# A six-layer cross network in bf16: the first layer as one sequence of twelve half-blocks

## The chip, the cores and the metric

The kernel runs on one core of a Trainium2 chip. The core has a matrix engine (TensorE, PE in the profile, with its weight loads shown as PEld), VectorE (DVE), ScalarE (ACT), GpSimd (POOL) and SyncE (SP), which here only issues DMAs. Engines run on their own instruction streams and wait for one another by semaphores. The metric is the device time of one execution in microseconds (us); lower is better.

## The reference

```python
B, F, D, L = 4096, 26, 16, 6          # Din = F * D = 416
x = x0                                 # (4096, 416) bf16
for l in range(6):
    x = x0 * (x @ ws[l] + bs[l]) + x   # ws (6, 416, 416), bs (6, 416)
return x
```

Each layer is a 4096x416 by 416x416 product, a bias, an elementwise product with the input and a sum.

## The kernel before

The data lie transposed: features on the 128 partitions, batch along the free dimension. The 416 features are three blocks of 128 (`m` as output block, `k` as input block) and a rest of 32. The batch is two parts `s` of 2048 columns, each part four groups of 512 (`g`), and a half `h` of a part is two groups (`gl` = 0, 1). A half-block (s, m, h) is 128 features by 1024 columns; it fills one PSUM tile [128, 2, 512] in fp32. The PSUM pool has four such buffers, which is the whole of PSUM, so a new tile waits until an older one has been read out.

The recurrence is kept as a running sum. In layer 0, `x0*(x0@W + b) + x0 = x0*(x0@W + b + 1)`, so 1 is added to layer 0's bias, `CM` holds the bracket, and `XH` holds `CM * XM0`, the next input. In a later layer the product is evicted into `t`, `CM += t`, and `XH = CM * XM0`. `CR`, `XR` are the same for the 32 rest features. There the four column groups of a part are stacked on the 128 partitions: partitions 32g to 32g+31 hold group g.

TensorE uses three shapes. A full product is 128x128 by 512 columns (layer 0, L240). A column-tiled product loads 32 output columns of the weights; four of them, on different quarters of the array, run side by side (layers 1 to 4, L208, and the rest features' output, `pr`, L220 and L224). A row-tiled product contracts only the 32 rest features; four of them, on partitions 0, 32, 64 and 96 of `XR` or `XRd`, run side by side (L214, and L247 in layer 0). `XRd` is `XR` with its halves of partitions swapped, so that the block m = 1 can use the other two quarters. Each 512 columns of a half-block take three full products (k = 0, 1, 2) and one row product.

Inputs. Eight DMA transposes on SP's queue bring `XM0` (512 columns each, in the order (s, g)). ScalarE's queue issues layer 0's weights, the biases, four pieces `xrig` (the rest columns of s = 0, turned by TensorE in `x0_rem0`), the rest rows of layer 0's weights `WR` (one quarter, copied to the other three by ScalarE twice and GpSimd once, L118 and L120), and `xrem` (the rest columns of s = 1, 2048 rows of 64 bytes, L91), which VectorE turns in `x0_rem1` (L172, L174). A memset of one column of `xrem` (L89), which VectorE does after the copies in `x0_rem0`, sets the moment at which this load is issued, since the DMA overwrites that column.

Order. Within an engine the order comes from the tile framework's scheduler, except where `pin` (keep in program order) fixes it. Layer 0 is `first_layer(s)`, called for s = 0 and s = 1. In each call the three half-blocks of h = 0 get their full products, then one group of eight row products runs (four half-blocks: (0,h=0), (0,h=1), (2,h=0), (1,h=0)), then the products of h = 1, then a group of four row products, so layer 0 has four row groups: eight, four, eight, four. For s = 0 the full products of half 0 are split around the four TensorE transposes of `x0_rem0`. At the end come the 32 products of `pr`. ScalarE evicts every tile (L181 in layer 0, L187 later, L194 and L197 for the rest); VectorE does all sums and products (L183, L188, L189, L198, L201).

Layers 1 to 4 take the tiles (s, m) two by two: 12 column-tiled steps, eight row products (closing one tile and opening the next), 12 steps; after the first pair comes the rest (`rem_pair`). The last layer works with the batch on partitions and writes the output; `xl_rem` copies the rest columns of the running sum, brought by a DMA transpose into `scrR`, for it.

Of the kernel before, what the change touches and what calls it, by code (L numbers as in the profile page):

```python
# [16 lines left out]
def kernel(  # L17
# [7 lines left out]
    nc = tc.nc  # L25
# [62 lines left out]
    def load_xrem1():  # L88
        pin(nc.vector.memset(xrem[:, 0, 0:1], 0.0))  # L89
        with nc.allow_non_contiguous_dma(reason="64B row segments"):  # L90
            pin(nc.scalar.dma_start(xrem[:], x0[SW:2 * SW, NK * P:D].rearrange("(p t) r -> p t r", p=P)))  # L91
# [23 lines left out]
    for g in range(1, NG):  # L115
        dst, src = WR[32 * g:32 * g + 32, 0, :], WR[0:R, 0, :]
        if g < NG - 1:
            nc.scalar.copy(dst, src)  # L118
        else:
            nc.gpsimd.tensor_copy(dst, src)  # L120
# [20 lines left out]
    fill_wd(0, 1)  # L141
    fill_wd(1, L)
# [33 lines left out]
    def ew_main(l, s, m, h, pt, nxt):  # L176
        c0 = col0(s, 2 * h)
        c, x = CM[:, m, c0:c0 + 2 * CW], nxt[s][:, m, 2 * CW * h:2 * CW * h + 2 * CW]
        src, bias = pt[:].rearrange("p a b -> p (a b)"), bM[:, m, l:l + 1]
        if l == 0:  # L180
            nc.scalar.activation(c, src, ACT.Identity, bias=bias, scale=1.0)  # L181
            for a in range(0, 2 * CW, CW):
                pin(nc.vector.tensor_tensor(out=x[:, a:a + CW], in0=c[:, a:a + CW],  # L183
                                            in1=XM0[:, m, c0 + a:c0 + a + CW], op=ALU.mult))
            return
        t = tpool.tile([P, 2 * CW], BF16, name="t")
        nc.scalar.activation(t[:], src, ACT.Identity, bias=bias, scale=1.0)  # L187
        nc.vector.tensor_tensor(out=c, in0=t[:], in1=c, op=ALU.add)  # L188
        nc.vector.tensor_tensor(out=x, in0=c, in1=XM0[:, m, c0:c0 + 2 * CW], op=ALU.mult)  # L189

    def ew_rem(l, s, pr, nxtR):
        cols = slice(CW * s, CW * s + CW)
        if l == 0:
            nc.scalar.activation(CR[:, cols], pr, ACT.Identity, bias=bR[:, 0:1], scale=1.0)  # L194
        else:
            tr = tpool.tile([P, 2 * CW], BF16, name="t")
            nc.scalar.activation(tr[:, 0:CW], pr, ACT.Identity, bias=bR[:, l:l + 1], scale=1.0)  # L197
            nc.vector.tensor_tensor(out=CR[:, cols], in0=tr[:, 0:CW], in1=CR[:, cols], op=ALU.add)  # L198
        for a in range(CW * s, CW * s + CW, CW if l else CW // 2):
            part = slice(a, a + (CW if l else CW // 2))  # L200
            prod = nc.vector.tensor_tensor(out=nxtR[:, part], in0=CR[:, part], in1=XR[0][:, part], op=ALU.mult)  # L201
            if l == 0:
                pin(prod)
# [14 lines left out]
    def mm_rem(l, s, pr, cur, curR):  # L218
        for g in range(NG):
            nc.tensor.matmul(pr[32 * g:32 * g + 32, :], lhsT=WD[:, l, g, :], rhs=curR[:, CW * s:CW * s + CW],  # L220
                             start=True, stop=False, tile_position=(0, 32 * g))
        for k in range(NK):
            for g in range(NG):
                nc.tensor.matmul(pr[32 * g:32 * g + 32, :], lhsT=WM[:, l, k, NK * P:D], rhs=cur[s][:, k, CW * g:CW * g + CW],  # L224
                      start=False, stop=(k == NK - 1), tile_position=(0, 32 * g))
# [8 lines left out]
    def first_layer(s):  # L234
        cur, curR, nxt, nxtR = XM0, XR[0], XH, XR[1]

        def full(pt, m, h, gl, after_row):
            c0 = col0(s, 2 * h + gl)
            for k in range(NK):
                nc.tensor.matmul(pt[:, gl, :], lhsT=WM[:, 0, k, 128 * m:128 * m + 128], rhs=cur[:, k, c0:c0 + CW],  # L240
                                 start=(k == 0 and not after_row), stop=(k == NK - 1 and after_row))

        def row(pt, m, h, opens):
            for gl in range(2):
                rg = 32 * ((2 * h + gl) ^ (2 if m == 1 else 0))
                src = XRd if m == 1 else curR
                nc.tensor.matmul(pt[:, gl, :], lhsT=WR[rg:rg + 32, 0, 128 * m:128 * m + 128],  # L247
                                 rhs=src[rg:rg + 32, CW * s:CW * s + CW],
                                 start=opens, stop=not opens, tile_position=(rg, 0))
# [3 lines left out]

        pa = [ph(m) for m in range(NK)]
        if s == 0:
            for m in range(NK):
                full(pa[m], m, 0, 0, False)
            tp0 = psum.tile([P, CW + 8], BF16, tag="ps", name="tpr")
            x0_rem0(tp0[:])
            for m in range(NK):  # L260
                full(pa[m], m, 0, 1, False)
        else:
            for gl in range(2):
                for m in range(NK):
                    full(pa[m], m, 0, gl, False)
        pb = [ph(0)]
        row(pa[0], 0, 0, False)
        row(pb[0], 0, 1, True)
        row(pa[2], 2, 0, False)
        row(pa[1], 1, 0, False)  # L270
        for m in range(NK):
            ew_main(0, s, m, 0, pa[m], nxt)
        for m in range(NK):
            if m:
                pb.append(ph(m))
            for gl in range(2):
                full(pb[m], m, 1, gl, m == 0)
        row(pb[1], 1, 1, False)
        row(pb[2], 2, 1, False)
        if s == 0:  # L280
            x0_rem1()
            for m in range(NK):
                ew_main(0, s, m, 1, pb[m], nxt)
            return
# [3 lines left out]
        for m in range(2):  # L288
            ew_main(0, s, m, 1, pb[m], nxt)
        ew_rem(0, 0, pr[:, 0, :], nxtR)  # L290
        ew_main(0, s, 2, 1, pb[2], nxt)
        ew_rem(0, 1, pr[:, 1, :], nxtR)
# [3 lines left out]
    for s in range(NS):  # L296
        first_layer(s)
# [10 lines left out]
    def xl_rem(s):  # L308
        tc.keep_in_program_order(
            nc.scalar.copy(XLrows[:, 16 * s:16 * s + 16, NK * P:D].rearrange("p (g i) r -> p i g r", g=NG),  # L310
                           scrR[s][:].rearrange("p i (g r) -> p i g r", g=NG)))
# [159 lines left out]
```

## Time and profile before

| | |
|---|---|
| time, median of 3 runs | 130.42 us (130.15 to 130.46) |
| the profiled execution's own time | 130.23 us |
| its span | 128.1 us |
| TensorE, matmuls | 123.5 us busy (96%), 1708 instructions |
| VectorE | 100.9 us (79%) |
| ScalarE | 86.2 us (67%) |
| GpSimd | 4.8 us (4%) |
| L208, column-tiled products | 65.2 us busy, 1152 instructions |
| L240, full products of layer 0 | 16.3 us busy, 379 ns each |
| L247, row products of layer 0 | 1.4% of the chain that ended last |

The page gives busy time by engine, the span in 40 slices (each digit is tenths of a slice, PEclk the clock granted to TensorE), the DMA queues (q1 is SP's, q10 ScalarE's), the chain of work that ended last, and the costliest groups of instructions. Matmuls overlap one another: a product of 512 columns is shown with 379 ns, but the next begins after a shorter step, so the step between starts is what counts. A timeline line gives start, length of the merged stretch, engine, line, operation, operands and count. "DMA to landing" is counted from the start of the issue.

### The profile page before, as it was taken

To read this page: it belongs to the slowest core of one execution; us is meant where nothing else is said; L and a number is where in the kernel's file an instruction comes from. 1 tells how busy PE (TensorE), PEld (TensorE's weight loads), DVE (VectorE), ACT (ScalarE), POOL (GpSimd) and SP (SyncE) were. 2 spreads that over 40 slices of the span, in tenths; PEclk is the share of its full clock that TensorE was granted. 3 is DMA by queue.
4 is the path that set the end of the run, shared out by engine and by line. 5 is a ranking of instruction groups with operands and counts; after the bars stand their busy time and mean duration, and the time that the engine had idled before them with its cause. 6 is when DMAs were issued, how large, how long until landed. Compare 5 with 4: busy or idle time off the path is not lost.

```text
span 128.1 us, 4002 instructions
## 1 busy us (share of the span) xinstructions
PE 123.5 (96%) x1708; PEld 55.9 (44%) x1710; DVE 100.9 (79%) x195; ACT 86.2 (67%) x98; POOL 4.8 (4%) x18
## 2 busy tenths in 40 slices
PE   7999999999999999999999999999999999999980
PEld 3343343444434444434444434444434445445450
DVE  0123579964979898989898989898989899988991
ACT  0048857878848668848668848668849696569660
POOL 4004001300000000000000000000000000000000
PEclk9999999999999999999999999999999999999999
DMA  3999999999940000000000000000498899976764
GB/s 93 234 234 224 174 238 259 318 332 336 336 144 0 5 0 0 8 0 5 0 5 0 5 0 5 0 0 5 86 125 192 161 135 236 199 231 220 228 194 142
DMA packets 42229, 16.37 MB, mean 128 GB/s; under 512 B 31034, under 2 KB 42212, under 8 KB 42212
## 3 DMA queue, kind: packets, MB, share of 16 engines
q1 hardware_dynamic: 37432, 15.40, 53.3%
q10 hardware_dynamic: 4780, 0.72, 3.6%
q8 instruction: 13, 0.21, 0.7%
q14 instruction: 4, 0.03, 0.1%
HBM read 6.15 MB, written 3.41 MB: 75 GB/s over the span
## 4 chain that ended last, share of the span: by engine, by line
PE 92%; DMA 4%; DVEq 1%; ACT 0%; issue 0%; DVE 0%
PE pt L208 50%; PE ph L240 13%; PE py L365 12%; PE pt L214 5%; PE pr L224 5%; DMA XM<-in_x_dram 4%; PE pr L220 2%; PE py L377 1%; PE ph L247 1%; PE py L380 1%; PE py L359 1%; DVEq L466 1%; PE tpr L163 1%; ACT t L405 0%; PE py L369 0%
## 5 line engine op out<-in xcount | busy, mean ns | idle before, releaser
L208 PE MATMUL pt<-XH,WM 128*32 128x512 bf16 x1152 | 65.2, 379 | 0.0
L187 ACT ACTIVATE t<-pt,bM 128x1024 bf16<-128x1024 f32 x48 | 49.6, 1115 | 19.3 <-PE pt L214 19.3
L208 PEld LDWEIGHTS <-WM 128*32 128x32 bf16 x1152 | 29.7, 97 | 33.8 <-issue 5.1
L188 DVE TENSOR_TENSOR CM<-t,CM 128x1024 bf16<-128x1024 bf16 x48 | 32.9, 686 | 5.1 <-ACT t L187 5.1
L189 DVE TENSOR_TENSOR XH<-CM,XM 128x1024 bf16<-128x1024 bf16 x48 | 33.2, 692 | 3.6
L405 ACT CAST t<-py 128x416 bf16<-128x416 f32 (+1 forms) x22 | 14.3, 649 | 5.1 <-PE py L365 2.0
L365 PE MATMUL py<-WM,XH 128*128 128x416 bf16 x90 | 17.0, 339 | 0.0
L240 PE MATMUL ph<-XM,WM 128*128 128x512 bf16 x70 | 16.3, 379 | 0.2
L181 ACT ACTIVATE CM<-ph,bM 128x1024 bf16<-128x1024 f32 x12 | 12.5, 1113 | 3.5 <-PE ph L247 3.5
L183 DVE TENSOR_TENSOR XH<-CM,XM 128x512 bf16<-128x512 bf16 x24 | 9.1, 438 | 3.6 <-ACT CM L181 3.6
L365 PEld LDWEIGHTS <-XH 128*128 128x128 bf16 x90 | 8.5, 98 | 7.6 <-issue 1.4
L240 PEld LDWEIGHTS <-WM 128*128 128x128 bf16 x72 | 6.8, 97 | 8.6 <-issue 1.1
L407 DVE TENSOR_TENSOR t<-t,XLrows 128x416 bf16<-128x416 bf16 (+1 forms) x20 | 9.3, 467 | 1.1 <-ACT t L405 1.1
L395 DVE TENSOR_TENSOR o<-t,X0rows 128x416 bf16<-128x416 bf16 (+1 forms) x22 | 9.9, 456 | 0.1
L214 PE MATMUL pt<-XR,WR 32*128 32x512 bf16 x96 | 7.3, 379 | 0.0
L224 PE MATMUL pr<-XH,WM 128*32 128x512 bf16 x96 | 6.6, 379 | 0.0
L197 ACT ACTIVATE t<-pr,bR 128x512 bf16<-128x512 f32 x8 | 5.1, 683 | 2.1 <-PE pr L224 2.1
L114 ACT ACT_TABLE_LOAD x1 | 1.3, 1283 | 6.1 <-DMA XM<-in_x_dram 6.1
L201 DVE TENSOR_TENSOR XR<-CR,XR 128x512 bf16<-128x512 bf16 (+1 forms) x12 | 4.4, 379 | 1.1 <-ACT CR L194 0.8
L224 PEld LDWEIGHTS <-WM 128*32 128x32 bf16 x120 | 3.2, 97 | 3.2
L148 PE MATMUL wps<-const-float32-1.0 128*128 128x512 f32 x4 | 3.8, 1094 | 0.8 <-PEq L455 0.8
L157 DVE CAST bM<-pb 128x18 f32<-128x18 bf16 x1 | 0.2, 177 | 4.9 <-PE pb L156 4.9
(52 smaller groups left out, 47.2 us busy)
## 6 DMA issues: line engine op xcount, KB each, us to landing
X0rows<-in_x_dram SPq DMA_DIRECT2D x8, 312.0 KB, 6.7
out_dram<-o SPq DMA_DIRECT2D x9, 208.0 KB, 3.2
WM<-in_ws_dram SPq DMA_DIRECT2D x5, 312.0 KB
out_dram<-o SPq DMA_DIRECT2D x13, 104.0 KB, 1.7
X0rows<-in_x_dram SPq DMA_DIRECT2D x4, 208.0 KB, 6.1
WR<-in_ws_dram SPq DMA_DIRECT2D x4, 130.0 KB, 4.8
WM<-in_ws_dram ACTq DMA_DIRECT2D x1, 312.0 KB
XM<-in_x_dram SPq DMA_TRANSPOSE x8, 5.7
```

Source lines behind the costliest of these rows:

```text
L181: nc.scalar.activation(c, src, ACT.Identity, bias=bias, scale=1.0)
L187: nc.scalar.activation(t[:], src, ACT.Identity, bias=bias, scale=1.0)
L188: nc.vector.tensor_tensor(out=c, in0=t[:], in1=c, op=ALU.add)
L189: nc.vector.tensor_tensor(out=x, in0=c, in1=XM0[:, m, c0:c0 + 2 * CW], op=ALU.mult)
L208: nc.tensor.matmul(pts[g // 2][32 * q:32 * q + 32, g % 2, :], lhsT=WM[:, l, k, 128 * m + 32 * q:128 * m + 32 * q + 32], rhs=cur[s][:, k, C ...
L214: nc.tensor.matmul(pts[g // 2][:, g % 2, :], lhsT=WR[32 * g:32 * g + 32, l, 128 * m:128 * m + 128], rhs=curR[32 * g:32 * g + 32, CW * s:CW ...
L224: nc.tensor.matmul(pr[32 * g:32 * g + 32, :], lhsT=WM[:, l, k, NK * P:D], rhs=cur[s][:, k, CW * g:CW * g + CW], start=False, stop=(k == NK ...
L240: nc.tensor.matmul(pt[:, gl, :], lhsT=WM[:, 0, k, 128 * m:128 * m + 128], rhs=cur[:, k, c0:c0 + CW], start=(k == 0 and not after_row), sto ...
L365: nc.tensor.matmul(py[:, 0:D], lhsT=q_x(q, g, k), rhs=WM[:, l, k, :], start=((not closes) and k == 0), stop=(closes and not adds and k == ...
L395: pin(nc.vector.tensor_tensor(out=o[:, 0:n, :], in0=src, in1=X0rows[:, b, :], op=ALU.mult))
L405: nc.scalar.copy(tv, src)
L407: pin(nc.vector.tensor_tensor(out=tv, in0=tv, in1=XLrows[:, rows(q, g0, n), :], op=ALU.add))
```

## The change

Layer 0 becomes one function without `s`. Its twelve half-blocks form one sequence with every instruction pinned, and three groups of eight row products. Write (s, m, h): the first group is as before. The second closes (0,1,1), (0,2,1), (1,0,0) and opens the second 512 columns of (1,1,0); the third closes (1,2,0), (1,0,1), (1,1,1) and opens (1,2,1). The last half-block (1,2,1) is finished by column-tiled products (`cols`), after which `pr` follows. Between the first and the second group stand the full products of (0,0,1), (0,1,1), (0,2,1), (1,0,0) and half of (1,1,0).

VectorE evicts half of (0,1,1) and the whole of layer 0's rest (`pr`); the products with `XM0` are placed by hand among the evictions. The load of `xrem` is released right after the four transposes, by a copy of one column of the transposes' tile in place of the memset, and is issued ahead of the copies of `WR`, which move into `x0_rem0`.

ScalarE evicts in halves: in layers 1 and 2 the two tiles of (s, m) = (0, 0) as 2 x 512 columns each, in all layers from 1 to 4 the rest as 2 x 256 per part, and `xl_rem(0)` copies in two pieces.

```diff
-    def load_xrem1():
-        pin(nc.vector.memset(xrem[:, 0, 0:1], 0.0))
+    def load_xrem1(tpr):
+        pin(nc.vector.tensor_copy(xrem[:, 0, 0:1], tpr[:, 3 * P:3 * P + 1]))
...
         for i in range(4):
             nc.tensor.transpose(tpr[:, 128 * i:128 * i + 128], xrig[:, i, :], ident[:])
+        load_xrem1(tpr)
+        copy_wr0()
...
-        load_xrem1()
...
     def ew_main(l, s, m, h, pt, nxt):
...
-        nc.scalar.activation(t[:], src, ACT.Identity, bias=bias, scale=1.0)
+        for a in range(2) if l < 3 and (s, m) == (0, 0) else (slice(0, 2),):
+            part = slice(a, a + 1) if isinstance(a, int) else a
+            nc.scalar.activation(t[:].rearrange("p (a b) -> p a b", a=2)[:, part], pt[:, part], ACT.Identity,
+                                 bias=bM[:, m, l:l + 1], scale=1.0)
...
     def ew_rem(l, s, pr, nxtR):
+        for a in range(0, CW, CW // 2):
+            nc.scalar.activation(t[:, a:a + CW // 2], pr[:, a:a + CW // 2], ACT.Identity, bias=bR[:, l:l + 1], scale=1.0)
...
+        def cols(pt, s, m, h, gl):
+            c0 = col0(s, 2 * h + gl)
+            for k in range(NK):
+                for q in range(4):
+                    pin(nc.tensor.matmul(pt[32 * q:32 * q + 32, gl, :], lhsT=WM[:, 0, k, 128 * m + 32 * q:128 * m + 32 * q + 32],
+                                         rhs=cur[:, k, c0:c0 + CW], start=False, stop=(k == NK - 1), tile_position=(0, 32 * q)))
...
+        x0_rem1()
+        for gl in range(2):
+            full(pb[0], 0, 0, 1, gl, False)
+        evict(pb[0], 0, 0, 1, both)
+        for m in range(1, NK):
+            pb.append(ph(m))
+            for gl in range(2):
+                full(pb[m], 0, m, 1, gl, True)
+        qa = [ph(0)]
+        for gl in range(2):
+            full(qa[0], 1, 0, 0, gl, True)
+        qa.append(ph(1))
+        full(qa[1], 1, 1, 0, 0, True)
+        row(pb[1], 0, 1, 1, ())
+        row(pb[2], 0, 2, 1, ())
+        row(qa[0], 1, 0, 0, ())
+        row(qa[1], 1, 1, 0, (1,))
+        evict(pb[1], 0, 1, 1, slice(0, 1))
+        evict(pb[1], 0, 1, 1, slice(1, 2), False)
+        evict(pb[2], 0, 2, 1, both)
+        evict(qa[0], 1, 0, 0, both)
+        product(0, 2, 0)
+        for m in range(NK):
+            product(0, m, 1)
+        product(1, 0, 0)
+        full(qa[1], 1, 1, 0, 1, False)
+        evict(qa[1], 1, 1, 0, both)
+        product(1, 1, 0)
+        qa.append(ph(2))
...
+        row(qa[2], 1, 2, 0, ())
+        row(qb[0], 1, 0, 1, ())
+        row(qb[1], 1, 1, 1, ())
+        row(qb[2], 1, 2, 1, (0, 1))
...
+        for gl in range(2):
+            cols(qb[2], 1, 2, 1, gl)
+        evict(qb[2], 1, 2, 1, both)
+        pr = psum.tile([P, 2, CW], FP32, tag="ps", name="pr")
+        for r in range(NS):
+            mm_rem(0, r, pr[:, r, :], [cur[:, :, 0:SW], cur[:, :, SW:B]], curR)
+        for r in range(NS):
+            part = slice(CW * r, CW * r + CW)
+            pin(nc.vector.tensor_scalar(out=CR[:, part], in0=pr[:, r, :], scalar1=bR[:, 0:1], scalar2=None, op0=ALU.add))
+            pin(nc.vector.tensor_tensor(out=nxtR[:, part], in0=CR[:, part], in1=XR[0][:, part], op=ALU.mult))
+        product(1, 2, 1)
...
     def xl_rem(s):
+        n = 4 if s else 2
+        for i in range(0, 4, n):
+            pin(nc.scalar.copy(dst[:, i:i + n], src[:, i:i + n]))
```

In the new function `qa` and `qb` are the PSUM tiles of s = 1, halves 0 and 1; `pa` and `pb` those of s = 0. `full(pt, s, m, h, gl, ...)` is three full products, `row(...)` two row products, `evict` an eviction of 1024 or 512 columns with the bias, `product` the two products with `XM0`.

More of the change, by code (lines that the diff above doesn't have):

```diff
@@ L266, in first_layer @@
[L266 to L270, printed above, removed]
-        for m in range(NK):
[L272 to L275, printed above, removed]
-            for gl in range(2):
[L277 to L284, printed above, removed]
+                pin(nc.tensor.matmul(pt[:, gl, :], lhsT=WR[rg:rg + 32, 0, 128 * m:128 * m + 128],
+                                     rhs=src[rg:rg + 32, CW * s:CW * s + CW],
+                                     start=gl in opens, stop=gl not in opens, tile_position=(rg, 0)))
```

131 lines of the change are left out of this document (71 added, 60 removed).

## The prediction

> **What bounds the kernel now.** I read the page first (engine shares, slices, chain), then TensorE's timeline through the first layer, then, for each thing TensorE will need earlier after the change, the timeline of ScalarE's and VectorE's queues and the DMA view. All times are from the start of the span.
>
> ```profile
> span 128.1 us, 4002 instructions
> ...
> PE 123.5 (96%) x1708; PEld 55.9 (44%) x1710; DVE 100.9 (79%) x195; ACT 86.2 (67%) x98; POOL 4.8 (4%) x18
> ...
> PE   7999999999999999999999999999999999999980
> ...
> PEclk9999999999999999999999999999999999999999
> DMA  3999999999940000000000000000498899976764
> ...
> PE 92%; DMA 4%; DVEq 1%; ACT 0%; issue 0%; DVE 0%
> ```
>
> TensorE is busy in every slice and carries 92% of the chain; the clock is full. So a microsecond that TensorE stands still is a microsecond of the kernel, and work taken off ScalarE or VectorE is worth nothing by itself. The DMA row is the warning: the engines that move data are full for the first eleven slices (35 us), just where the change asks for data earlier.
>
> ```profile
> 11.38 4.06 PE L240 MATMUL ph<-XM,WM 128*128 128x512 bf16 x17
> 15.37 0.39 PE L247 MATMUL ph<-XRd,WR 32*128 32x512 bf16 x2
> 15.38 0.39 PE L247 MATMUL ph<-XR,WR 32*128 32x512 bf16 x2
> 15.70 4.06 PE L240 MATMUL ph<-XM,WM 128*128 128x512 bf16 x18
> 19.69 0.60 PE L247 MATMUL ph<-XR,WR 32*128 32x512 bf16 x6
> 19.92 0.38 PE L247 MATMUL ph<-XRd,WR 32*128 32x512 bf16 x2
> 20.23 4.06 PE L240 MATMUL ph<-XM,WM 128*128 128x512 bf16 x17
> ...
> 24.55 0.40 PE L220 MATMUL pr<-XR,WD 128*32 128x512 bf16 x4
> ...
> 26.28 2.76 PE L208 MATMUL pt<-XH,WM 128*32 128x512 bf16 x48
> ```
>
> Here is the price list. The 18 full products from 15.70 to 19.69 take 3.99; 18 steps of 0.216 are 3.89, so entering a row group costs 0.10. Eight row products (19.69 to 20.23) take 0.54 where two steps of four together are 0.43: leaving costs 0.11. One visit to row tiling thus costs 0.21 beyond its steps. From `pr` at 24.55 to 26.28 there are 8 column-tiled steps, 1.73, and no switch to the next layer. No stall is seen.
>
> ```profile
> 10.46 0.63 ACTq L91 DMA_DIRECT2D xrem<-in_x_dram  x1
> ...
> 16.95 2.36 DVE L172 STREAM_TRANSPOSE XR<-xrem 128x512 bf16<-128x512 bf16 x1 [1.22 <-DMA xrem<-in_x_dram]
> 19.34 0.61 DVE L174 COPY XRd<-XR 64x512 bf16<-64x512 bf16 x2
> ```
>
> The second half's rest columns: issued at 10.46, landed 6.4 later, transposed at 16.95, the first `XRd` copy done at 19.63 (19.34 plus half of 0.61). The row group at 19.69 came just after.
>
> **The change part by part.**
>
> *Three row groups instead of four.* Same 72 products, 24 row products, eight `pr` steps; six steps of the last half-block become column-tiled, at the same 0.216 a step (12 steps of L208 from 26.28 take 2.6). One visit goes: **-0.21**. Without stalls I place the new order from 11.38 on: 27 steps and one entry put the second group at 17.31, its second half (the two half-blocks of s=1) at 17.53; it resumes at 17.85, 21 steps and an entry give the third group at 22.49, the column-tiled steps begin at 23.04 and layer 1 at 26.07 against 26.28.
>
> *The xrem load moved ahead.* Its guard becomes a copy from `tpr`, the first VectorE work after the transposes (8.74 before) in place of a memset at 10.37. It costs between 0.06 (that memset) and 0.17 (the copy of `bR` from the same tile); I take 0.16, being the same kind of read. `XR` and `XRd` for s=0 are late by that, done at 10.22 instead of 10.06, and the first group needs them at 10.72 and 11.07: hidden. The load issues at 8.95, 1.5 earlier. Behind it on ScalarE's queue stand the two `WR` copies, which started at 9.69 when their DMA landed; the issue's 0.63 ends at 9.58, so this adds 0 (0.1 if cover fails). On SP's queue nothing changes order; POOL's `WR` and `WD` copies are needed only by the row group and `pr`, and still wait for the same landing.
>
> *What the second row group now waits for.* Two of its half-blocks are of s=1, so it needs the transposed rest columns at 17.53, where before they were needed at 19.69 to 19.92: 2.2 earlier, while the load is issued only 1.5 earlier. From landing to TensorE it takes 0.10 + 2.36 + 0.03 + 0.29 + 0.04 = 2.82, so the load must land by 14.71 to cost nothing. When does it? Lower bound: the pieces of `xrig`, a quarter as large, take 4.2 from issue to landing, giving 13.2 and no stall. Same latency as before, 6.4: 15.35, a stall of 0.64. Upper bound by sharing:
>
> ```profile
> q1 hardware_dynamic: 717, 0.18, 91.6%
> q10 hardware_dynamic: 637, 0.04, 48.2%
> ```
>
> This is the DMA view from 13.75 to 14.75: SP's queue (q1, the transposes) and ScalarE's (q10, 2048 packets of xrem) share. Before, xrem began 3.0 after its issue (13.49), shared for a microsecond, and then had the engines nearly alone as the transpose beside it ran out (1399 packets in 14.75 to 15.65); its last packet went at 15.6. Moved, it begins near 11.98 with two transposes ahead of and beside it, so the free stretch comes late or never. At 637 a microsecond throughout, 2048 packets take 3.2, end at 15.2 and land 1.25 later (as 15.6 to 16.85 before): 16.4, a stall of 1.7. I take 15.75, between the two rows of this very transfer and nearer the first, since the transpose beside it will thin out at some point: **+1.03**, ends 0 and 1.7.
>
> The Trainium skill (DMA: Bandwidth & Descriptors, section Queues, rings and completion order) says that each DMA engine alternates between the queues that have work. The 717 and 637 agree; by that rule alone the load lands at the late end, an estimate of 132.0 in all, which is a rival below.
>
> *Data for s=1 wanted earlier.* The old order took the first 512 columns for all three m, then the second; the new one finishes half-block (1,0,0), both column blocks, first. Block (1,0) is needed at 15.27 (before 15.70) and landed at 13.7; fine. Block (1,1) is needed at 15.92, before at 17.65.
>
> ```profile
> L78 SPq DMA_TRANSPOSE XM<-in_x_dram x1: 2041/2041/2041, 10.4 to 10.4; - x1
> ...
> DMA to landing us min/median/max: 6.6/6.6/6.6
> ```
>
> It landed at 16.93, beside xrem. If nothing moves it, TensorE stops there for 1.06; if xrem's 1.3 to 2.1 of engine time now falls partly on the transpose before it, it lands at 15.5 to 16.2 and costs 0 to 0.3. I take 0.2, but add nothing: this stop comes first and shortens the row group's wait by as much. The sum takes the larger of the two.
>
> *Evictions in the first layer.* After the second group, tile `qa[2]` needs `pb[1]`'s buffer three steps later, at 18.48. The buffer is freed by ScalarE's half (0.69, as L194's 128x512) and VectorE's half. VectorE reading fp32 from PSUM is seen once,
>
> ```profile
> L395 DVE TENSOR_TENSOR o<-py,X0rows 128x416 bf16<-128x416 f32 x1 | 0.6, 583 | 0.0
> ```
>
> which scaled to 512 columns is 0.72 at most; the bf16 copy of 512 is 0.42; I take 0.69. Started at 17.74 it ends at 18.43: just in time. But if the group was held by `XRd`, VectorE still has its second copy (0.32) to do, and is 0.09 late: **+0.09** (0 to 0.15). Queued behind it are the products of (0,2,0) and the six of half 1, needed only at layer 1, some 7 us later.
>
> *Rest columns of layer 0 evicted by VectorE.* By ScalarE they ended at 27.9 before. Now VectorE does the product of (1,1,1) until 26.8, then 0.69 + 0.42 + 0.69 to 28.65. `XR1` of s=0 is ready at 27.95, needed at 28.72; the `pr` buffer is free at 28.69, needed at 28.93. Cover 0.2, cost 0 (0.2 if VectorE reads at 0.8). Where TensorE is late, all of this shifts with it.
>
> *Halves on ScalarE in layers 1 and 2, and in every rest pair.* Two 512s step by 0.57 each against 1.01 for one 1024: +0.13 per tile, +0.26 per pair of tiles; four 256s by extrapolation 0.35 each against two 0.57: +0.27. ScalarE waits 1.5 us for TensorE ahead of each pair of tiles and 0.5 ahead of the rest pair; VectorE gets its operands 0.3 later against 5 us of slack. Cost 0. The split copy of `scrR` adds about 0.2 in front of a 1.1 wait: 0.
>
> Sum against the profiled run's 130.23 (span 128.1, 2.1 around it): -0.21 + 1.03 + 0.09 = +0.91, or 131.14. The median of the runs, 130.42, lies 0.19 above the profiled run, so I forecast **131.3**.
>
> **Rivals.** *No stop at all (not slower).* If the load, begun under a transpose already two thirds done, goes as the `xrig` pieces did, it lands by 14.7 and block (1,1) by 15.9; then only the -0.21 counts: 130.2. For it: the DMA engines had slow stretches (486 packets from 12.45 to 13.45 against about 1130 a microsecond at best) that an earlier load could fill. Against: 14.7 is 5.75 after issue, and this transfer took 6.4. It decides at 15.2: later, and the kernel is over 0.3% slower, which is about what a measurement here can tell from no change. *Even sharing*: 130.42 - 0.21 + 1.7 + 0.09 = 132.0; for it the packet counts, against it the free stretch at the end of the old load. *Block (1,1) stays at 16.93*: TensorE stops 1.06 in the six products of (1,0,0), the row group finds its columns ready: 131.3, the same time for another reason. For it: the same bytes must still pass ahead of it.
>
> **How the numbers follow.** Held at the row group 46%, even sharing 13%, held by block (1,1) 8%: slower 67%. No stop to speak of: 33%, of which 6% for a time more than 0.3% below (130.0), which the -0.21 alone doesn't reach, and 27% same. The range runs from 130.1 (no stop) to 132.1 (late end); for the slower cases alone 130.8 to 132.1.
>
> **What would show it.** In the changed profile: three groups of eight row products in layer 0, a gap in TensorE at the s=1 half of the second (near 17.5) ended by VectorE's `XRd` copy, the xrem load issued near 8.95, the stream transpose starting near 15.85 behind a DMA wait, layer 1 starting near 27.2. I am wrong if that transpose starts before 14.8, if the gap is in the products of (1,0,0), or if TensorE waits in layers 1 to 4 on ScalarE's halves.

## The result and the profile after

The changed kernel takes 130.78 us in the median of 20 runs (130.42 to 131.62); the kernel before, on the same chip, 130.22 in 20 runs (130.04 to 130.54). The ratio is 1.0047, 95% interval 1.0033 to 1.0061: slower by 0.56 us. The profiled execution took 130.64.

From the page of the changed kernel: the span, the busy times, two rows of the slices, and the chain.

```profile
span 128.8 us, 4051 instructions
...
PE 123.8 (96%) x1727; PEld 55.9 (43%) x1728; DVE 102.6 (80%) x196; ACT 86.4 (67%) x109; POOL 4.9 (4%) x18
...
PEclk9999999999999999999999999999999999999999
DMA  3999999999950000000000000000398999975764
...
PE 95%; ACT 1%; DVE 1%; DVEq 1%; issue 0%
```

The bound and the clock are as before. What differs lies in layer 0. TensorE's timeline of the changed kernel (start, length of the merged stretch, engine, line, operands, count; in brackets the idle time just before and what ended it):

```profile
10.82 0.60 PE L255 MATMUL ph<-XR,WR 32*128 32x512 bf16 x6
...
11.51 6.00 PE L239 MATMUL ph<-XM,WM 128*128 128x512 bf16 x26
17.45 0.39 PE L255 MATMUL ph<-XRd,WR 32*128 32x512 bf16 x2
17.45 0.60 PE L255 MATMUL ph<-XR,WR 32*128 32x512 bf16 x4
17.68 0.38 PE L255 MATMUL ph<-XRd,WR 32*128 32x512 bf16 x2
17.99 0.82 PE L239 MATMUL ph<-XM,WM 128*128 128x512 bf16 x3
19.40 4.04 PE L239 MATMUL ph<-XM,WM 128*128 128x512 bf16 x18 [0.59 <-DVE CM L266]
23.38 0.40 PE L255 MATMUL ph<-XR,WR 32*128 32x512 bf16 x4
...
23.92 1.48 PE L248 MATMUL ph<-XM,WM 128*32 128x512 bf16 x24
...
26.95 0.39 PE L200 MATMUL pt<-XH,WM 128*32 128x512 bf16 x4
```

The second row group runs from 17.45 to 17.99: 0.54, the price of a group that waits for nothing. The stop foretold there is absent. Three products later stands a stop that was foretold at 0.09. The product before the gap starts at 18.43 and the next at 19.40, a step of 0.970 where 0.216 is usual: 0.754 lost. (The profile's 0.59 counts from the modelled end of a product, so steps between starts are used here.) The same view for VectorE and ScalarE:

```profile
14.58 2.36 DVE L174 STREAM_TRANSPOSE XR<-xrem 128x512 bf16<-128x512 bf16 x1 [0.42 <-DMA xrem<-in_x_dram]
16.98 0.61 DVE L176 COPY XRd<-XR 64x512 bf16<-64x512 bf16 x2
18.60 0.75 DVE L266 TENSOR_SCALAR CM<-ph,bM 128x512 bf16<-128x512 f32 x1 [1.01 <-ACT CM L264]
```

```profile
9.10 0.62 ACTq L91 DMA_DIRECT2D xrem<-in_x_dram  x1
9.83 1.10 ACT L139 COPY WR<-WR 32x416 bf16<-32x416 bf16 x2 [2.07 <-DMA WR<-in_ws_dram]
17.88 3.70 ACT L264 ACTIVATE CM<-ph,bM 128x512 bf16<-128x512 f32 x4 [2.49 <-PE ph L255]
```

Here is the loss. VectorE was done with `XRd` at 17.59, and its half of (0,1,1) was complete in PSUM with the row group. But it starts at 18.60, 1.01 idle, released by ScalarE's eviction: ScalarE's half ran from 17.88 for 0.69, to 18.57. The two halves of one tile were evicted one after the other. VectorE's ended at 19.35, and `qa[2]` got the buffer then.

Counted from the end of the first row group to the end, the profiled executions took 116.76 before and 117.31 after: +0.56. The row group that is gone (-0.21) and the stop (+0.754) come to +0.54.

The rest of the account lies elsewhere. Each execution has its time and its span. The median span is 129.0 (128.6 to 129.8) against 128.1 to 128.2 for the kernel before: about +0.87. The time outside the span is 1.78 in the median against 2.10: -0.32. The two make up the +0.56, to rounding.

### The profile page after: what moved, and what is told of

Its sections match the earlier page's. It is cut to its first block, busy times and chain, and to the rows that moved or that the text cites. A ratio compares the mean times of both kernels' runs of the same rounds, so it can differ in the third digit from the quotient of the medians.

```text
span 128.8 us, 4051 instructions
## 1 busy us (share of the span) xinstructions
PE 123.8 (96%) x1727; PEld 55.9 (43%) x1728; DVE 102.6 (80%) x196; ACT 86.4 (67%) x109; POOL 4.9 (4%) x18
## 4 chain that ended last, share of the span: by engine, by line
PE 95%; ACT 1%; DVE 1%; DVEq 1%; issue 0%
PE pt L200 49%; PE py L422 12%; PE ph L239 11%; PE pt L206 5%; PE pr L220 5%; PE wps L149 4%; PE pr L216 2%; PE py L434 1%; PE ph L255 1%; PE py L437 1%; PE ph L248 1%; PE py L416 1%; DVE CM L266 1%; DVEq L523 1%; ACT CM L264 1%; ACT t L462 0%
## 5 line engine op out<-in xcount | busy, mean ns | idle before, releaser
L184 ACT ACTIVATE t<-pt,bM 128x1024 bf16<-128x1024 f32 (+1 forms) x52 | 50.2, 1051 | 18.7 <-PE pt L206 18.7
L239 PE MATMUL ph<-XM,WM 128*128 128x512 bf16 x65 | 15.0, 379 | 0.6 <-DVE CM L266 0.6
L264 ACT ACTIVATE CM<-ph,bM 128x1024 bf16<-128x1024 f32 (+1 forms) x12 | 12.0, 1080 | 5.1 <-PE ph L255 5.1
L239 PEld LDWEIGHTS <-WM 128*128 128x128 bf16 x66 | 6.2, 98 | 8.5 <-issue 1.7
L193 ACT ACTIVATE t<-pr,bR 128x256 bf16<-128x256 f32 x16 | 6.3, 475 | 1.6 <-PE pr L220 1.6
L216 PE MATMUL pr<-XR,WD 128*32 128x512 bf16 x40 | 3.9, 379 | 0.0
```

What stands on the lines that cost most here:

```text
L184: nc.scalar.activation(t[:].rearrange("p (a b) -> p a b", a=2)[:, part], pt[:, part], ACT.Identity, bias=bM[:, m, l:l + 1], scale=1.0)
L239: mm = nc.tensor.matmul(pt[:, gl, :], lhsT=WM[:, 0, k, 128 * m:128 * m + 128], rhs=cur[:, k, c0:c0 + CW], start=(opens and k == 0), stop=( ...
L264: pin(nc.scalar.activation(c, src, ACT.Identity, bias=bias, scale=1.0))
```

## The experiments

Theory **T**: the whole loss is the stop for `pb[1]`'s buffer, and the stop is that long because VectorE's half waits for ScalarE's. Rivals: **R1**, the halves added to ScalarE in layers 1 to 4; **R2**, the early load and what it displaces; **R3**, late data (xrem or block (1,1)). The ratios below are of whole times; a table at the end of this section sets the spans beside them.

**ScalarE evicts (0,1,1) whole** (5 rounds).

```diff
-        evict(pb[1], 0, 1, 1, slice(0, 1))
-        evict(pb[1], 0, 1, 1, slice(1, 2), False)
+        evict(pb[1], 0, 1, 1, both)
```

> The changed kernel with one edit undone: the tile of (0,1,1) is evicted whole by ScalarE (1024 columns) instead of half by ScalarE and half by VectorE. Buffer theory: in the changed kernel's trace VectorE's half begins only when ScalarE's half is done (18.60 after 17.88 + 0.69), so the two halves take 1.47 in series; TensorE stands 0.75 waiting for that buffer. Whole on ScalarE it takes 1.11, so the wait falls to about 0.39 and the time by 0.36: from 0.56 us above the kernel before to about 0.20 above (ratio near 1.0015). Rival, data theory: the gap of the profile is chance and the timed runs lose their time to late rest columns of s=1; then the time stays about 0.5 us above (ratio 1.004) and the wait at the second row group shows.

Measured: 1.0009 [0.9993, 1.0025]. TensorE's timeline of this kernel:

```profile
17.80 0.82 PE L239 MATMUL ph<-XM,WM 128*128 128x512 bf16 x3
18.86 2.10 PE L239 MATMUL ph<-XM,WM 128*128 128x512 bf16 x9 [0.23 <-ACT CM L264]
```

The step is 0.610, so 0.39 is lost where 0.754 was. One engine alone frees the buffer sooner than two that share it.

**VectorE evicts it whole** (5 rounds): `evict(pb[1], 0, 1, 1, both, False)` in place of the two lines.

> The changed kernel with the tile of (0,1,1) evicted whole by VectorE, 1024 columns in one instruction. Buffer theory: VectorE's 512 took 0.75, so 1024 take about 1.28 at its rate of 0.53 per 512 more; no series with ScalarE, and the wait at the buffer is 1.28 - 0.69 - 0.04 = about 0.55 instead of 0.75: time 0.2 below the changed kernel, 0.36 above the kernel before (ratio 1.003). Data theory: as the changed kernel, 1.004 to 1.005.

Measured: 1.0012 [1.0, 1.0025], a step of 0.784 (0.57 lost). VectorE and ScalarE of this kernel:

```profile
17.75 1.28 DVE L266 TENSOR_SCALAR CM<-ph,bM 128x1024 bf16<-128x1024 f32 x1 [0.18 <-PE ph L255]
```

```profile
17.79 3.12 ACT L264 ACTIVATE CM<-ph,bM 128x1024 bf16<-128x1024 f32 x3 [2.46 <-PE ph L255]
```

This run narrows down what makes the engines take turns. VectorE reads `pb[1]` from 17.75 while ScalarE reads `pb[2]` from 17.79, both released by TensorE. They write the same tile `CM`, in different columns, as the two halves do. So neither `CM` as a whole nor PSUM as a whole orders them. What the halves share beyond that is the PSUM tile they read, and the block m = 1 of `CM`, in which they write different columns. I take it to be the PSUM tile; no run separates the two.

**The halves swapped** (3 rounds): VectorE takes the first 512 columns and stands first in the program, ScalarE the second.

```diff
-        evict(pb[1], 0, 1, 1, slice(0, 1))
-        evict(pb[1], 0, 1, 1, slice(1, 2), False)
+        evict(pb[1], 0, 1, 1, slice(0, 1), False)
+        evict(pb[1], 0, 1, 1, slice(1, 2))
```

> The changed kernel with the two halves of the tile of (0,1,1) in the other order: VectorE evicts the first 512 columns, ScalarE the second. If the program makes two engines that read one PSUM tile take turns, whichever comes first, ScalarE's half begins when VectorE's ends, at 17.85 + 0.75 = 18.60, and ends at 19.29 + 0.04: the same wait of 0.70 to 0.75, now ended by ScalarE, and the same time as the changed kernel (ratio 1.004). If only VectorE's place in the order matters, the halves overlap, the wait falls to 0.1 and the time to 0.1 below the kernel before.

Measured: 1.0043 [1.0028, 1.0058]. VectorE, ScalarE and TensorE of this kernel:

```profile
17.95 0.75 DVE L266 TENSOR_SCALAR CM<-ph,bM 128x512 bf16<-128x512 f32 x1 [1.07 <-PE ph L255]
```

```profile
18.74 2.70 ACT L264 ACTIVATE CM<-ph,bM 128x512 bf16<-128x512 f32 x3 [3.62 <-DVE CM L266]
```

```profile
16.13 1.46 PE L239 MATMUL ph<-XM,WM 128*128 128x512 bf16 x6 [0.22 <-DMA XM<-in_x_dram]
...
19.48 1.24 PE L239 MATMUL ph<-XM,WM 128*128 128x512 bf16 x5 [0.59 <-ACT CM L264]
```

Now ScalarE, idle for 3.62, waits for VectorE. The releaser has changed sides and the step is 0.971, the same. The order comes from the program, not from one engine being late: in the trace VectorE's half waits for ScalarE's semaphore in the changed kernel, and here ScalarE's half waits for VectorE's. (At 16.13 this run also waited for block (1,1); more on that below.)

**The later halves undone** (5 rounds): one 1024 eviction in layers 1 and 2, one 512 for each rest part, `xl_rem` in one piece; layer 0 as changed.

```diff
-        for a in range(2) if l < 3 and (s, m) == (0, 0) else (slice(0, 2),):
+        for a in (slice(0, 2),):
...
-        n = 4 if s else 2
+        n = 4
```

> The changed kernel with ScalarE's later halves undone (layers 1 to 4 and the copy of scrR as in the kernel before); the first layer stays as changed. Both theories: TensorE waits for no eviction in layers 1 to 4, so the time is the changed kernel's within 0.1 us (ratio to the kernel before 1.004 to 1.005). Rival: the 0.3 us that the halves add to ScalarE per layer reach TensorE; then the time falls by 0.3 or more.

Measured: 1.0056 [1.0036, 1.0076], and the same stop (19.42, 0.59 idle by VectorE's half). Its median span is 129.0, that of the changed kernel, so within the span the halves in layers 1 to 4 neither cost nor gain; R1 falls. (That its ratio is the larger comes from outside the span: 1.95 there instead of 1.78.)

**The early load alone, in the kernel before** (5 rounds).

```diff
-    def load_xrem1():
-        pin(nc.vector.memset(xrem[:, 0, 0:1], 0.0))
+    def load_xrem1(tpr):
+        pin(nc.vector.tensor_copy(xrem[:, 0, 0:1], tpr[:, 3 * P:3 * P + 1]))
...
+        load_xrem1(tpr)
+        copy_wr0()
...
-        load_xrem1()
```

> The kernel before with one part of the change: the load of the rest columns of s=1 released right after the transposes, ahead of the WR copies. The first layer keeps its old order, which needs those columns only at 19.7. Both theories: no wait is taken away, so no gain; within 0.1 us of the kernel before (ratio 1.000). Rival: the load ahead of the WR copies holds the first row group, or the moved DMA makes a transposed block of s=1 late; then 0.1 to 0.3 us slower, and the first row group starts later or a gap shows in the products of (1,0,0).

Measured: 0.9987 [0.9978, 0.9997]. Not slower, so R2 falls as far as the old order can show it (there the blocks of s=1 are needed later); the next experiment tests the load in the new order. But it is some 0.2 us faster, which I had not expected. From the end of the first row group on, its profile takes 116.78, as before, and its median span is 128.2, as before. The gain is outside the span: 1.77 in the median, 2.10 in the kernel before. The last experiment takes that up.

**The late load, in the changed kernel** (3 rounds): the guard is again a memset behind the copies in `x0_rem0`, so the load is issued at 10.40.

> The changed kernel with the load of the rest columns of s=1 released as late as in the kernel before (the memset after the XRd copies, issue near 10.5 instead of 9.1). Buffer theory and data theory agree that the row group then waits: columns landed at 16.85 with that issue, the first XRd copy done at 19.63, the group's s=1 half placed at 17.6, so TensorE waits about 2.0 there; VectorE then has its second copy to do before it can evict, so the wait for the buffer shrinks to 0.1 to 0.2. In all about 2.0 us above the kernel before (132.2 us, ratio 1.015). If the load would land as fast as in the changed kernel, 5.4 us after its issue, it would be 1.0 less (131.2).

Measured: 1.0114 [1.0098, 1.013], +1.45 us. VectorE and TensorE of this kernel:

```profile
16.70 2.34 DVE L174 STREAM_TRANSPOSE XR<-xrem 128x512 bf16<-128x512 bf16 x1 [2.70 <-DMA xrem<-in_x_dram]
19.08 0.61 DVE L176 COPY XRd<-XR 64x512 bf16<-64x512 bf16 x2
19.72 0.75 DVE L266 TENSOR_SCALAR CM<-ph,bM 128x512 bf16<-128x512 f32 x1
```

```profile
16.64 1.46 PE L239 MATMUL ph<-XM,WM 128*128 128x512 bf16 x6 [0.65 <-DMA XM<-in_x_dram]
18.03 0.39 PE L255 MATMUL ph<-XRd,WR 32*128 32x512 bf16 x2
...
19.10 0.39 PE L255 MATMUL ph<-XR,WR 32*128 32x512 bf16 x2 [0.67 <-DVE XR L174]
19.42 0.39 PE L255 MATMUL ph<-XRd,WR 32*128 32x512 bf16 x2
```

Here both waits of the prediction stand: 0.81 for block (1,1) (a step of 1.030 to 16.64) and 0.84 for the rest columns in the s=1 half of the second group (1.056 to 19.10), 0.10 more because the second copy of `XRd` comes a step after the first, and 0.12 three products later for the buffer, as VectorE starts its half at 19.72 when ScalarE's is long done. The wait at the group is below the 2.0 expected, since TensorE comes to it 0.81 later and the load landed at 16.61, not 16.85. So the mechanisms were there, and the early load gains rather than loses in the new order, which ends R2. The load issued 1.3 earlier keeps the wait for the rest columns away; the wait for block (1,1) is absent from both profiles of the changed kernel, but stands in two kernels with the early load (halves swapped, three copies).

**More cover behind the second group** (5 rounds): ScalarE evicts (0,1,1) whole, and two of the three products of (1,1,0)'s first 512 columns follow the second group instead of preceding it, so that `qa[2]` comes five products behind it, not three.

```diff
...
-        full(qa[1], 1, 1, 0, 0, True)
+        full(qa[1], 1, 1, 0, 0, True, ks=(0,))
...
-        row(qa[1], 1, 1, 0, (1,))
-        evict(pb[1], 0, 1, 1, slice(0, 1))
-        evict(pb[1], 0, 1, 1, slice(1, 2), False)
+        row(qa[1], 1, 1, 0, (1,), (0,))
+        evict(pb[1], 0, 1, 1, both)
...
+        full(qa[1], 1, 1, 0, 0, False, ks=(1, 2))
```

> As the run before, and two of the three full products of the first 512 columns of (1,1,0) moved behind the second row group, so that five steps instead of three stand between the group and the tile that waits for the buffer. Buffer theory: the wait falls by another 0.43 to about 0; the group comes 0.43 earlier, its s=1 half at about 17.24, where the XRd copy was done at 17.27: 0.05 to 0.1 there. Time about 0.1 us below the kernel before (ratio 0.999). Data theory: the columns are wanted 0.43 earlier and were late already, so the time rises to 0.9 us above the kernel before (ratio 1.007).

Measured: 0.999 [0.998, 1.0001], 130.08 us, and no stop for the buffer; the products behind the second group run on without a gap:

```profile
16.92 0.60 PE L255 MATMUL ph<-XR,WR 32*128 32x512 bf16 x4
17.20 0.39 PE L255 MATMUL ph<-XRd,WR 32*128 32x512 bf16 x2
17.53 3.41 PE L239 MATMUL ph<-XM,WM 128*128 128x512 bf16 x15
```

From the end of the first row group its profile takes 116.63: 0.13 less than before, close to the 0.21 less the 0.07 that the second group is longer. But the median span, 128.25, is no shorter than before. What takes the gain back in the timed runs is not shown; the profiled execution itself has a span of 128.0.

**A third engine for the `WR` copies** (5 rounds): as the kernel above, and one of ScalarE's two `WR` copies goes to VectorE, behind its `XRd` copies (GpSimd's copies of `WD` from `WR` move along in the program).

```diff
...
+            if g == 2:
+                continue
...
-        fill_wd(0, 1)
-        fill_wd(1, L)
...
+        pin(nc.vector.tensor_copy(WR[64:96, 0, :], WR[0:R, 0, :]))
+        fill_wd(0, 1)
+        fill_wd(1, L)
```

> The version without the wait (whole eviction by ScalarE, two more products behind the second row group) and one of the two WR copies moved from ScalarE to VectorE, behind its XRd copies. In its trace ScalarE's two copies end at 10.83 and the first row group takes 0.72 where later groups take 0.54. With one copy each on ScalarE, VectorE and GpSimd they end near 10.4, so the group should take 0.54 to 0.6: 0.12 to 0.17 less, 0.25 to 0.3 below the kernel before (ratio 0.998). If the group is held by something else, the time is that of the version before it (0.999).

Measured: 0.9979 [0.9969, 0.999], 130.07 us (129.62 to 130.38). TensorE of this kernel:

```profile
10.69 0.60 PE L258 MATMUL ph<-XR,WR 32*128 32x512 bf16 x6
10.92 0.38 PE L258 MATMUL ph<-XRd,WR 32*128 32x512 bf16 x2
11.23 4.06 PE L242 MATMUL ph<-XM,WM 128*128 128x512 bf16 x18
...
16.55 1.02 PE L242 MATMUL ph<-XM,WM 128*128 128x512 bf16 x4 [0.61 <-DMA XM<-in_x_dram]
17.50 0.39 PE L258 MATMUL ph<-XRd,WR 32*128 32x512 bf16 x2
```

The first row group lasts 0.54, not 0.72 as in the kernel above (0.59 to 0.72 in every profile with two copies on ScalarE): it had waited for the second `WR` copy. But TensorE then reaches block (1,1) sooner, and in this execution the block landed late: 0.77 lost at 16.55.

**Block (1,1) used later** (5 rounds): the products ahead of the second group are reordered so that (1,1) is first used 0.65 later; two products of (1,0,0) follow the group instead of two of (1,1,0), and the group keeps its place.

```diff
-        for gl in range(2):
-            full(qa[0], 1, 0, 0, gl, True)
+        full(qa[0], 1, 0, 0, 0, True)
...
-        full(qa[1], 1, 1, 0, 0, True, ks=(0,))
+        full(qa[1], 1, 1, 0, 0, True)
+        full(qa[0], 1, 0, 0, 1, True, ks=(0,))
...
-        row(qa[0], 1, 0, 0, ())
-        row(qa[1], 1, 1, 0, (1,), (0,))
+        row(qa[0], 1, 0, 0, (), (1,))
+        row(qa[1], 1, 1, 0, (1,))
...
+        full(qa[0], 1, 0, 0, 1, False, ks=(1, 2))
...
-        full(qa[1], 1, 1, 0, 0, False, ks=(1, 2))
```

> This is e9_three_copies with the order of the first layer's products changed: block (1,1) is first used about 0.65 us later (at about 16.57 instead of 15.92 after the start), while the second row group stays where it is. Theory A, block (1,1) sometimes lands late and that makes the spread of the timed runs: in e9 it landed at 16.50 in one profile and at 15.7 to 15.8 in others, so up to 0.6 us of waiting disappears from the runs that had it. The spread of e9 (129.62 to 130.38) shrinks to about 0.4 us, the median is about 129.9, the ratio about 0.996 to 0.997. Theory B, the spread has another source (the start-up alone): ratio 0.998 as in e9, spread as wide. By both there is no gap of TensorE at the second row group and none at block (1,1) in a profile where it lands before 16.5.

Measured: 0.9974 [0.9961, 0.9987], 130.08 us (129.71 to 130.19). The interval holds both theories' ratios, and the spread of 0.48 against 0.76, in 9 and 12 runs, decides nothing either. What the profile shows I had said would not be there. VectorE, then TensorE:

```profile
14.85 2.35 DVE L177 STREAM_TRANSPOSE XR<-xrem 128x512 bf16<-128x512 bf16 x1 [0.82 <-DMA xrem<-in_x_dram]
17.23 0.61 DVE L179 COPY XRd<-XR 64x512 bf16<-64x512 bf16 x2
```

```profile
16.73 0.91 PE L258 MATMUL ph<-XR,WR 32*128 32x512 bf16 x4
17.57 0.39 PE L258 MATMUL ph<-XRd,WR 32*128 32x512 bf16 x2
17.90 0.82 PE L242 MATMUL ph<-XM,WM 128*128 128x512 bf16 x3
```

The second group takes 1.17 instead of 0.54: with the group at 16.73, the s=1 half waits for `XR` (ready at 17.20) and then `XRd` (17.52). That is the prediction's stop at the second group, 0.63 long, with a transpose that starts at 14.85. The gain of the shorter first group is handed back to a load once more. Both kernels have a median span of 128.3, no shorter than the kernel before; moving the group itself later without losing the cover behind it wasn't tried.

**Both kernels once more**, a profile each.

> The changed kernel as it is, for a second profile. Buffer theory: again one gap of about 0.75 after the second row group, ended by VectorE's half eviction. Data theory: the gap is at the s=1 half of the row group or in the products of (1,0,0), ended by a DMA or the XRd copy.

> The kernel before as it is, for a second profile: no gap in TensorE in the first layer; the rest columns land 6.4 us after their issue again; the start of the first product and the time around the span show how far two profiles of one kernel differ (0.1 to 0.5 us expected).

The changed kernel shows the same stop (0.754 at 19.34, ended by VectorE's half), the kernel before none.

**ScalarE's halves alone, in the kernel before** (5 rounds): the halves of layers 1 to 4 (without `xl_rem`), nothing else.

```diff
-        nc.scalar.activation(t[:], src, ACT.Identity, bias=bias, scale=1.0)
+        for a in ((0, CW), (CW, 2 * CW)) if l < 3 and (s, m) == (0, 0) else ((0, 2 * CW),):
+            nc.scalar.activation(t[:, a[0]:a[1]], src[:, a[0]:a[1]], ACT.Identity, bias=bias, scale=1.0)
...
-            nc.scalar.activation(tr[:, 0:CW], pr, ACT.Identity, bias=bR[:, l:l + 1], scale=1.0)
+            for a in range(0, CW, CW // 2):
+                nc.scalar.activation(tr[:, a:a + CW // 2], pr[:, a:a + CW // 2], ACT.Identity, bias=bR[:, l:l + 1], scale=1.0)
```

> The kernel before, with only ScalarE's halves in layers 1 to 4 (two 512s for the tiles (0, 0) of layers 1 and 2, two 256s for each rest part). It asks for two things. First, whether the halves are worth anything within the span: from the end of the first row group on I expect 116.75 as before, since ScalarE waits for TensorE ahead of each of these evictions, and a span of 128.1 to 128.2. Second, where 0.3 us outside the span come from: the time minus the span was 2.05 to 2.16 in every run of the kernel before, 1.77 to 1.81 in the median of every kernel with the new layer 0 and of the early load alone, and 1.95 in the one with the later halves undone. Theory A, it belongs to the moved WR copies (the one edit that all the others share): it stays at 2.10 here, ratio 1.000. Theory B, it follows from the program as a whole, any edit can move it: it changes, by -0.17 if the difference of 1.95 and 1.78 carries over, to 1.93, ratio 0.9987.

Measured: 0.9979 [0.9968, 0.9989], 130.02 us. The span is 128.2 in the median, as before (128.2 beside it), and 116.77 from the end of the first row group. Outside the span it spends 1.79 (1.74 to 1.83) where the kernel before spends 2.05 to 2.15 in the runs beside it. Theory A falls: the `WR` copies are where they were. An edit that changes nothing within the span, by the profile, moves the time outside it by 0.3, and each program keeps its own value: 2.1 before, 1.95 with the later halves undone, 1.77 to 1.81 for the other ten. What in a program sets it is open; neither the number of instructions (4002 give 2.1, 4005 give 1.77, 4051 give 1.78) nor any one part of the change does.

The stops of each profile, added to the span before (128.15) and -0.21 for the missing row group (and -0.12 in the last two lines, where the first group takes 0.54 instead of 0.66), against the median spans:

| kernel | stops in its profile, us | span by the sum | median span | outside | ratio of times |
|---|---|---|---|---|---|
| before | none | | 128.1 to 128.2 | 2.10 | 1 |
| as changed | 0.754 | 128.7 | 129.0 | 1.78 | 1.0047 [1.0033, 1.0061] |
| halves swapped | 0.755 (and 0.38 for the block) | 128.7 | 129.05 | 1.81 | 1.0043 [1.0028, 1.0058] |
| later halves undone | 0.756 | 128.7 | 129.0 | 1.95 | 1.0056 [1.0036, 1.0076] |
| whole on VectorE | 0.57 | 128.5 | 128.6 | 1.78 | 1.0012 [1.0, 1.0025] |
| whole on ScalarE | 0.39 | 128.3 | 128.5 | 1.78 | 1.0009 [0.9993, 1.0025] |
| more cover | 0.07 | 128.0 | 128.25 | 1.80 | 0.999 [0.998, 1.0001] |
| late load | 0.81 + 0.84 + 0.10 + 0.12 | 129.8 | 129.95 | 1.79 | 1.0114 [1.0098, 1.013] |
| three copies | none (and 0.77 for the block) | 127.8 | 128.3 | 1.80 | 0.9979 [0.9969, 0.999] |
| block (1,1) later | 0.63 | 128.45 | 128.3 | 1.81 | 0.9974 [0.9961, 0.9987] |

From the late load (129.95) down to the whole eviction on ScalarE (128.5) the median spans follow the stops, and where the stop is gone (more cover) 0.75 of the 0.87 is gone too. So theory T holds for the greater part of the loss, but not for the whole: the medians lie 0.1 to 0.35 above the sums (0.5 with three copies, and 0.15 below with block (1,1) later), and the three lowest kernels are not in the order of their sums. Late landings in part of the runs (R3) would do that, but the timed runs without a profile don't show it. No kernel of the study has a span shorter than the kernel before by more than its spread; those that are 0.2 to 0.3% faster are so outside it.

## Why the prediction was right, and where its steps failed

The direction was right and the size near: +0.56 against the +0.9 forecast, and +0.87 if only the span is taken, which is all that the prediction reckoned with. But the reason put first was not the reason. The stop on which the sum rests (1.03) did not occur, another that was put at 0.09 cost 0.754, and 0.32 came off outside the span, where nothing was foretold. That these misses add up to a time near the forecast is luck.

- *Three row groups instead of four, -0.21*: right from the end of the first group on (116.63 with more cover, where the second group is 0.07 longer, and 116.76 before). It never became a shorter median span.
- *What the second row group now waits for, +1.03*: this step failed. The load was issued at 9.10 (8.95 foretold) and the transpose began at 14.58; with the 0.10 between the two that the prediction used it landed at 14.48, 5.4 after its issue. I had taken 15.75. The first copy of `XRd` was done at 17.27 and needed at 17.67: 0.4 to spare, the term was 0. By the prediction's own criterion (the transpose before 14.8) the step is wrong. What failed in it is the time of landing; the wait itself is real where the columns come late: with the late load the stop was 0.84 and with the group 0.7 earlier 0.63, each where the arithmetic of 2.82 from landing to TensorE puts it (14.75 landed + 2.82 = 17.57, when the `XRd` product started in the last experiment).
- *Why it landed early.* I had let xrem share with block (1,1) at 637 packets a microsecond to the end. In the changed kernel's trace its first packet went at 11.57 and its last at 13.53. The DMA view of 12.0 to 12.6, then that of 12.6 to 13.2:

```profile
q1 hardware_dynamic: 452, 0.12, 85.3%
q10 hardware_dynamic: 454, 0.03, 52.2%
```

```profile
q10 hardware_dynamic: 1165, 0.07, 133.6%
q1 hardware_dynamic: 109, 0.02, 17.8%
```

  In the first stretch the two queues share evenly. In the second SP's queue moves almost nothing, and xrem goes alone, at some 1940 packets a microsecond. The free stretch of the old load, which I had expected late or never, came again. It was block (1,0), a transpose earlier than I had thought, that shared with xrem: it landed at 14.4 instead of 13.6, still ahead of its need. Of the 1.0 by which the load was faster from issue to landing (5.4 against 6.4), 0.56 is the wait for its first packet (2.47 against 3.03), 0.15 the transfer (1.96 against 2.11) and 0.3 the time from the last packet to landing. The Trainium skill (DMA: Bandwidth & Descriptors, section Queues, rings and completion order) says that a DMA engine alternates between the queues that have work. The 454 and 452 agree with it; what the late end assumed beyond it, that SP's queue has work to the end, is what did not hold.
- *Evictions in the first layer, +0.09*: the term that was mis-sized, 0.754 measured. The prediction named the place, the tile and the buffer, but let VectorE's half start beside ScalarE's at 17.74. It started at 18.60, behind it. The step "the buffer is freed by ScalarE's half and VectorE's half" is a sum of the two (0.69 + 0.75), not the longer one. In the late-load kernel, where VectorE was held by `XRd` anyway, the term was 0.12.
- *Block (1,1), 0.2 not added*: needed at 16.06, landed at 15.81, nothing lost in this execution. But it landed at 15.7 to 16.6 in the kernels derived from the changed one, and cost 0.38, 0.77 and 0.81 in three of their profiles. With the early load the traces show a pattern. In three profiles (halves swapped, three copies, block (1,1) later) ScalarE issued xrem 0.03 to 0.09 before SP issued the transpose of block (1,0); xrem's first packet then went 1.55 after its issue, and block (1,1) landed at 16.1 to 16.5. In the six others with the new order xrem was issued at most 0.02 before that transpose, or after it; its first packet went 2.5 to 2.7 after its issue, and the block landed at 15.7 to 15.8 (16.0 in the early load alone, in the old order). So which of two issues comes first, by less than 0.1, seems to decide; no run sets that order on purpose. That may make the wide spread of the changed kernel's spans (128.6 to 129.8, against 127.9 to 128.4 with the block used later); it was not shown, since no profile of the changed kernel itself has that wait.
- *`WR` copies, 0 (0.1 if cover fails)*: the cover held in this execution and failed in the second profile. Here the issue ended at 9.72, but `WR` itself landed only at 9.80 (9.67 before), and the copies began at 9.83, as soon behind the landing as before. In the second profile `WR` landed at 9.65, the issue ended at 9.72 and the copies began at 9.77, so it held them by 0.09. The first group ended 0.13 later than before (11.51 against 11.38) in the first profile, as much as `WR` landed later. That this group waits for the copies is shown by the three-copies kernel.
- *`pr` by VectorE, 0*: right. The two evictions took 0.75 and 0.74 and ended at 29.51, all shifted with TensorE.
- *ScalarE's halves in layers 1 to 4, 0*: right within the span, by the kernel without them and by the halves alone. In the changed kernel's profile the view of waits has one line for TensorE from 11 to 27, and none from 25 to 100:

```profile
PE ph L239 <- DVE CM L266: 0.6, 1, 0.6
```

- *A term that the prediction did not have*: -0.32 outside the span. It set the sum against the profiled run's 130.23, "span 128.1, 2.1 around it", and let the 2.1 stand. It is a value of the program, and it changed with the program. Without it the time would have been 131.1.

The rival *even sharing* was right for half a microsecond and wrong to the end, *no stop* was right on the load and wrong on the time, and *block (1,1)* is real in some runs but not the cause.

## What to carry to other kernels

Splitting the eviction of one PSUM tile between two engines frees its buffer later, not sooner, where the program makes the two engines take turns, as it did here: look whether the second reader's releaser is the first one. Give the engines different tiles, and count how many products lie between a tile's last product and the next use of its buffer; here five hid an eviction of 1024 columns and three did not. Compare spans as well as times: two kernels here differ by 0.2% and have the same span. When work on the bounding engine is shortened or reordered, list every load by landing time and need: here two of the reordered kernels ran into a late load in their profiles (0.77 and 0.63).

## What the runs showed of the hardware that I had not expected

- VectorE reads fp32 from PSUM at 0.75 us for 128x512 and 1.28 for 128x1024, ScalarE at 0.69 and 1.11. When the two read different tiles at the same time (whole on VectorE), ScalarE took 1.11 as elsewhere; VectorE's 1.28 is that same run's, and no run has it alone.
- The same load of 2048 rows of 64 bytes went from issue to the transpose that reads it in 5.1 (halves swapped, 8.76 to 13.89, where VectorE took it up without a wait), 5.5 (9.10 to 14.58), 5.9 (with block (1,1) used later), 6.1 (the kernel before, once more), 6.3 (late load) and 6.5 us (the kernel before). A margin of 0.4 on it is luck.
- The time outside the span keeps to one value in each program, within 0.13, and changes by 0.15 to 0.3 with edits that leave the span alone (2.10, 1.95 and 1.78). Effects of 0.2% on a kernel of this length can be that and nothing else.
- The start varies from profile to profile: the first row group began anywhere from 10.55 to 10.90 after the span's start. Counting from the end of the first row group took that out.
